# No-ops of the half pairs on four queues, later loads freed from the transposes, and a new order of steps

## The chip, the cores and the metric

The kernel runs on one core of a Trainium2 chip. A core has five engines with a queue of instructions each: TensorE (PE in the profile; its weight loads are listed apart as PEld), VectorE (DVE), ScalarE (ACT), GpSimd (POOL) and SyncE (SP). Here SP computes nothing: it issues transfers and holds no-ops. The metric is the time of one execution on the device, in microseconds. The profile's times count from the start of the span, the first instruction of the profiled execution; a clock of 1.00 is TensorE at full speed.

## What is computed

Two branches on the same normalised input, multiplied, and added to the input. S = 2048 tokens, D = 448, 16 heads of 28, F = 1792.

```
xn  = layernorm(x)                                  # no scale, no bias
q, k, v = heads of (xn @ wqkv)
idx = pos - 2 * (0 .. 7)                            # window 8, dilation 2
o   = softmax(q . k[idx] / sqrt(28), idx < 0 masked) @ v[idx]
s   = o @ wo                                        # branch A
f   = gelu(xn @ w1 + b1) @ w2 + b2                  # branch B
out = x + s * silu(f)
```

All inputs are bf16. A token attends only to tokens of its own parity.

## The kernel before

**Tiles and stages.** The tokens are split by parity into two halves of 1024 and cut into 16 tiles of 128: t0 to t7 are the even tokens, t8 to t15 the odd ones. Four tiles make one of the chunks c0 to c3, the 512 columns that a matmul of the hidden layer takes. Per tile: VectorE takes statistics of x_sb (line 353) and aggregates them; the inverse root follows (rstds; from t4 on on POOL, lines 374 and 375, two or four tiles at a time); VectorE normalises; and xn is turned into xnT, for t0 to t3 by TensorE, from t4 on by a transposing transfer that SP issues (dma_T, line 300). From xnT come Q and K of the tile (line 478), which are copied from a PSUM bank into qk_tok or qk_pair (line 251) and turned into qkT by another transposing transfer, and V (line 501), which POOL stores into v_rows in DRAM and loads back in strips for the attention (line 294). The hidden layer (ff1, line 551) takes one chunk of xnT and one of 14 column tiles of w1, m0 to m13; ACT applies gelu. The second layer (ff2) is line 577 for c0 to c2 and line 603 for c3. The attention works on nine blocks b0 to b8 of up to 228 tokens, each in two parts: keys (line 662), scores (line 677), exponential, mask (line 693), weighted sum of the values (line 708). The last part multiplies by wo (line 742), gates, adds x and stores.

**Pairs.** A contraction of 448 rows is three tiles of 128 and one of 64. The function pair takes two such jobs a and b with a PSUM bank each and runs their matmuls on the two row halves of the array at once: first a on rows 0 to 63 beside b on rows 64 to 127 (the first half of the pair), then with the row halves exchanged (the second half). Between the two stands a no-op on another engine's queue (line 437): it waits for the last matmuls of the first half, and the second half waits for it. So there are three steps: first half, no-op, second half. Before, the no-op is on POOL or on SP, and for pairs marked early (the projections and the hidden layer of c0 and c1) on POOL alone: 49 stand on POOL, 12 on SP.

**The order.** Every piece of work is a step of a plan (plan.add) with a number, the engines that may carry it, the steps that it depends on, and the buffers that it takes and gives back. emit walks through the string ORDER and issues the steps in its order. A word is an engine's letter and the step's number: P TensorE, V VectorE, A ACT, G POOL, S SP, D for a transfer's landing. Words of one letter are that engine's queue, which it works off in this order; buffers (the eight PSUM banks, the four buffers for xn among them) are handed out in the order of the words, so that a step can also wait for an earlier user of its buffer.

**Loads.** x comes in parts: t0, t1, t2 and t3, t4 to t7, and, by load_x(8, 4) and load_x(12, 4), t8 to t11 (step S256) and t12 to t15 (S258), 0.46 MB each. w2 comes in two halves, S262 and S260. These four depend on the issue of the xn transposes of t4 to t7 (the list turned, line 851), so that they stand behind them on SP's queue; so does the load of the bias b2 on POOL (G264).

**Steps that are spoken of.**
- Transposes on SP: S196, S200, S188, S192 turn xn of t6, t7, t4, t5; S137, S154, S144, S161 turn Q and K of t0, t2, t1, t3; S425 of t13.
- Pairs (first half, no-op, second half): V of t6 and t7 P239, 240, 241; Q and K of t4 P202, 203, P204, of t5 P209, 210, P211, of t6 P225, 226, P227, of t7 P232, 233, P234, of t10 P362, 363, P364, of t14 P436, 437, P438. Hidden layer of c0: P303, 304, P305 and P313, 314, P315, and further ones numbered 288 to 322. Hidden layer of c1: P472, 473, P474; P477, 478, P479; P482 and P502 are first halves of others, P487, P489, P497, P499 halves too. Second layer: P577, P579. The no-ops 217 and 340 belong to V of t4 and t5 and of t8 and t9, 444 to V of t14 and t15.
- Attention: scores P652, P657, P682, P687, P692; P782 is the weighted sum of b4, first part.
- VectorE: V281 is the statistic of t13, V229 the copy of Q of t6 out of its bank, V331 the normalisation of t10.
- POOL: G96 inverse root of t4 and t5; G278 and G287 those of t8 to t11 and of t12 to t15; G172 to G178 loads of values for b0, G180 and G182 for b1, G385 to G391 for b4; G357 the store of V of t8.

Of the kernel before, what the change touches and what calls it, by code (L numbers as in the profile page):

```python
# [11 lines left out]
ACT = mybir.ActivationFunctionType  # L12

HOPS = ("POOL", ("SP", "POOL"))
# [4 lines left out]
G98 P5 S40 D41 S44 D45 P6 S46 D47 P7 G100 P8 V58 P9 V59 S74 D75 V62 A60 P10 S76 D77 P11 V61 V102 P12 P13 G649 V103 P14  # L19
V63 P104 A64 P105 G27 V106 A107 D108 S78 D79 G28 V65 P128 G31 V109 G29 V110 G30 P111 P112 V113 S80 D81 P132 A114 D115  # L20
P129 S84 D85 V66 P184 P133 V67 V70 A68 S86 D87 P130 V69 V116 P131 V117 V71 V185 P118 V101 A72 P119 V99 A52 V120 D121
# [12 lines left out]
A685 G233 G661 V711 A584 P234 S363 V684 A242 P687 G920 G686 V236 P364 A235 V585 P586 A688 S237 D238 G243 D244 A690  # L34
V689 G246 D247 A581 G691 S921 D922 A366 V582 S923 D924 A365 P712 S367 D368 G587 P692 P662 V693 A713 P588 V663 V694
A715 V664 V695 V665 V696 V666 G697 D698 P346 V589 G667 D668 S669 D670 P717 V592 A590 G347 P671 G699 D700 P348 V672
A718 G252 D253 V673 P413 A349 G254 D255 V350 A720 P339 G414 V674 S351 D352 V675 A593 P415 G340 V740 G676 D677 P701
V714 A417 P341 G678 D679 V702 A416 V703 P595 A343 S418 D419 V716 V704 A342 V705 V741 G706 D707 S344 D345 V594 G708
D709 P722 V719 G596 P742 V723 P747 V724 A743 P597 S925 D926 A745 V725 V726 A748 V721 G727 D728 S729 D730 A750 V591
V744 V746 P731 V601 P376 V732 A602 V733 P369 G377 V734 P378 V735 G370 P353 V598 G738 S736 D737 D739 A382 S927 D928  # L40
V770 A599 P752 G383 D384 P371 V753 G354 V379 P355 A372 V754 G380 D381 P427 A356 V771 A359 P443 G357 D358 V755 V756
G360 D361 P772 V373 S444 S757 D758 P445 G428 G759 D760 A773 V749 S374 D375 P777 A775 V446 P429 A778 V751 P420 V800
# [3 lines left out]
A440 V784 V785 V786 G460 D461 G462 D463 V439 S789 G787 D788 D790 V806 S441 D442 G459 P807 V610 P537 A808 V607 A810  # L46
P791 S538 P812 V809 A54 G464 D465 P512 V792 V793 G466 D467 P539 V794 S513 V795 A608 P514 V813 G798 S796 D797 D799 V814
A541 S931 D932 P527 V815 A540 V816 P532 G528 V811 A515 G817 D818 V609 G819 D820 P821 A611 P529 V860 G533 G468 D469
A516 V822 P534 V823 G470 D471 A531 P507 V824 V825 A536 V612 P522 G826 D827 S828 D829 A530 G508 A535 P509 S523 A861
P517 P952 S518 A511 P524 G953 A510 S933 D934 P954 A525 P519 V955 A526 P941 V959 G956 A521 V960 P832 P837 A520 G942  # L50
S957 D958 P943 S961 D962 A55 P613 V944 V948 V949 A838 S950 D951 A840 V839 V945 A833 P862 V841 S946 D947 G614 P867 A835
V834 P615 A868 V836 A870 G869 A863 A865 V864 G871 A890 P842 V619 P622 G866 V843 V844 A620 V845 A891 V846 V616 G847
D848 V621 P851 G849 D850 A617 S623 P892 P624 V852 A893 V853 A895 V854 V855 V618 G856 D857 V894 G858 D859 V896 P547
V628 V625 P963 A629 G548 A626 V630 P897 G964 P974 A898 V627 A900 P965 V899 G975 A56 V901 P542 S935 D936 V970 P976 V971
G543 V966 S972 D973 P549 V977 G967 P902 A551 P544 V903 V904 S968 D969 A550 P552 V905 V978 A546 V906 S979 D980 P872
G553 P554 A545 V981 S907 D908 P881 S909 D910 V873 A556 P572 V874 A555 V882 P567 V883 S573 V884 V885 P574 S568 V875
G886 D887 P569 V876 A575 G888 D889 V982 P996 A576 G877 D878 S983 D984 P557 A571 G997 G879 D880 A570 P998 S558 P911
V999 P559 V912 P562 V913 A560 V1000 A561 P985 V914 S563 S1001 D1002 V915 P564 S937 D938 V1003 G986 G918 P987 V1004
A565 P631 S1005 D1006 V992 A566 S916 D917 D919 V988 A57 V993 P632 V989 S994 D995 S990 D991 P635 V633 A634 S939 D940
P1012 P636 P1007 V637 P639 A638 V1008 V1009 V1013 S1010 D1011 P640 G1014 P643 S1015 D1016 V641 A642 P644 P1022 A645  # L60
P1017 V1023 V1024 P646 V1018 S1025 D1026 P647 P1027 V1019 A648 V1028 S1020 D1021 V1029 S1030 D1031
# [61 lines left out]
def kernel(  # L123
# [12 lines left out]
    nc = tc.nc  # L136
    P = 128
# [795 lines left out]
```

## Time and profile before

| | us |
|---|---|
| three timed runs | 155.18, 153.72, 155.64 |
| their median | 155.18 |
| the profiled execution's own time | 155.25 |
| its span, first to last instruction | 153.6 |
| mean granted clock of TensorE | 1.000 |

The profile is of one execution. In its rows, L437 is a line of the kernel, an arrow points from the inputs to the output (out<-in), xN is a count. SPq and POOLq are the queues of SP and POOL, whose no-ops and issues of transfers are not counted as work. The busy time of the engines by stretch shows how the work is spread (the columns: start and end, length, busy us and instructions of each engine, TensorE's clock, mean busy share of the transfer engines, GB/s):

```
0.00:20.00 20.00, 18.00 (x130) 9.02 (x132) 15.57 (x58) 8.70 (x17) 10.30 (x38) 1.00 0.97 254
20.00:40.00 20.00, 18.40 (x176) 9.32 (x174) 10.07 (x31) 12.12 (x20) 7.94 (x13) 1.00 1.10 206
40.00:60.00 20.00, 18.14 (x262) 9.73 (x258) 14.39 (x33) 12.71 (x24) 11.45 (x15) 1.00 1.01 175
60.00:80.00 20.00, 20.00 (x370) 11.45 (x364) 19.01 (x51) 10.33 (x22) 8.28 (x15) 1.00 0.94 153
80.00:100.00 20.00, 18.86 (x298) 10.71 (x296) 17.71 (x49) 12.28 (x24) 13.16 (x23) 1.00 1.08 201
100.00:120.00 20.00, 20.00 (x304) 10.69 (x300) 12.96 (x30) 16.29 (x30) 7.83 (x11) 1.00 0.34 86
120.00:140.00 20.00, 20.00 (x248) 10.36 (x243) 15.48 (x37) 13.84 (x23) 3.61 (x6) 1.00 0.37 102
```

The five engines' columns are TensorE, its weight loads, VectorE, ACT and POOL. The last stretch, from 140.00 to 153.60, is not shown.

### The profile page before, as it was taken

Reading aid. Unit: us, or ns where it says so; the run is one execution under the profiler, and the core shown is the slowest. Engines: PE = TensorE matmul, PEld = TensorE weight load, DVE = VectorE, ACT = ScalarE, POOL = GpSimd, SP = SyncE. Lnnn points to the kernel's source line nnn. Section 1 sums busy time; section 2 is a strip of 40 time slices with the busy share of each in tenths; the row PEclk is TensorE's granted clock in tenths of the full one; section 3 lists DMA queues with packets and bytes.
Section 4 is the critical chain, followed back from the end, with each engine's and each line's share of the span. In section 5 each row is a group of like instructions: output and inputs, shape, how many; then the busy total and the mean of one; then the engine's idle time right before and its main releaser. Section 6 shows DMA issues by size and latency. Waiting matters only on the chain.

```text
span 153.6 us, 4656 instructions
## 1 busy us (share of the span) xinstructions
PE 143.6 (94%) x1828; PEld 77.4 (50%) x1828; DVE 110.2 (72%) x295; ACT 88.5 (58%) x161; POOL 63.6 (41%) x119
## 2 busy tenths in 40 slices
PE   6999999977999959999999889999999999999991
PEld 2554555533455526556555446545555555445560
DVE  5689962068845795999999959925869999481542
ACT  3253576693485574374367227998895775672120
POOL 6833396002918490453274864742084022210200
PEclk9999999999999999999999999999999999999999
DMA  4999999999599898979689999981601242353301
GB/s 145 343 329 287 165 200 153 277 227 258 103 230 178 164 157 188 113 182 156 143 109 275 136 174 224 227 192 22 180 0 41 57 107 68 101 145 90 89 30 60
DMA packets 43950, 24.28 MB, mean 158 GB/s; under 512 B 33778, under 2 KB 41978, under 8 KB 43928
## 3 DMA queue, kind: packets, MB, share of 16 engines
q1 hardware_dynamic: 41080, 17.25, 58.7%
q0 software_dynamic: 2704, 6.62, 17.8%
q8 instruction: 14, 0.23, 0.7%
q10 hardware_dynamic: 144, 0.11, 0.2%
q14 instruction: 8, 0.07, 0.2%
HBM read 9.82 MB, written 6.29 MB: 105 GB/s over the span
## 4 chain that ended last, share of the span: by engine, by line
PE 64%; DMA 17%; DVE 11%; POOL 2%; issue 2%; SPq 1%; ACT 0%; POOLq 0%; DVEq 0%
PE bank L551 16%; PE bank L577 16%; PE bank L478 8%; PE bank L603 7%; DMA xnT<-xn 6%; PE bank L742 5%; DMA x_sb<-in_A_x_dram 5%; PE bank L501 4%; DMA v<-v_rows 4%; PE bank L264 3%; PE bank L708 3%; DVE kb L662 3%; DVE st L353 3%; DMA qkT<-qk_pair 2%; PE bank L677 2%
## 5 line engine op out<-in xcount | busy, mean ns | idle before, releaser
L551 PE MATMUL bank<-xnT,w 64*128 64x512 bf16 x392 | 47.3, 376 | 0.8 <-DVE qk_tok L251 0.8
L555 ACT ACTIVATE h<-bank,b 128x512 bf16<-128x512 f32 x56 | 35.2, 685 | 16.4 <-PE bank L551 16.0
L577 PE MATMUL bank<-w,h 64*128 64x448 bf16 x336 | 33.7, 349 | 0.0
L551 PEld LDWEIGHTS <-w 64*128 64x128 bf16 x392 | 20.3, 94 | 20.6 <-issue 1.8
L478 PE MATMUL bank<-w_in,xnT 64*128 64x448 bf16 (+1 forms) x212 | 26.8, 352 | 3.6 <-SPq L437 2.6
L683 ACT ACTIVATE E<-bank 128x456 bf16<-128x456 f32 (+1 forms) x36 | 17.4, 550 | 12.3 <-PE bank L677 10.2
L731 POOL DMA_DIRECT2D o_rows<-a x25 | 13.4, 540 | 25.1 <-DVE a L724 10.0
L577 PEld LDWEIGHTS <-h 64*128 64x128 bf16 x336 | 16.1, 94 | 13.9
L724 DVE TENSOR_TENSOR a<-bank,rd 114x448 bf16<-114x448 f32 (+1 forms) x36 | 22.2, 622 | 1.1
L294 POOL DMA_DIRECT2D v<-v_rows x22 | 13.6, 627 | 10.6 <-DMA v_rows<-v_tok 6.0
L478 PEld LDWEIGHTS <-xnT 64*128 64x128 bf16 (+1 forms) x212 | 10.3, 94 | 12.7 <-SPq L437 2.8
L353 DVE BATCH_NORM_STATS2 st<-x_sb 128x6 f32<-128x448 bf16 x16 | 9.5, 612 | 8.2 <-DMA x_sb<-in_A_x_dram 8.2
L501 PE MATMUL bank<-w_in,xnT 64*128 64x448 bf16 (+1 forms) x106 | 14.1, 351 | 0.0
L619 DVE TENSOR_TENSOR y<-bank,b 128x448 f32<-128x448 f32 x15 | 9.0, 621 | 6.3 <-PE bank L603 4.8
L294 POOL DMA_DIRECT2D v_rows<-v_tok x16 | 9.2, 576 | 7.4 <-DVE v_tok L251 4.6
L603 PE MATMUL bank<-w,h 128*128 128x448 bf16 (+2 forms) x70 | 11.4, 315 | 0.0
L693 POOL TENSOR_TENSOR E<-E,m_gen 128x456 bf16<-128x456 bf16 x8 | 8.5, 1076 | 6.4 <-ACT E L683 6.4
L631 ACT ACTIVATE t<-y 128x448 f32<-128x448 f32 x12 | 6.9, 579 | 7.2 <-DVE y L619 7.2
L662 DVE TENSOR_SCALAR kb<-qkT,plane 128x512 bf16<-128x512 bf16 x30 | 10.7, 410 | 0.2 <-DMA qkT<-qk_pair 0.2
L773 POOL TENSOR_TENSOR o<-x_sb,sg 128x448 bf16<-128x448 bf16 x3 | 3.1, 1030 | 17.8 <-DVE sg L767 9.1
L387 DVE TENSOR_SCALAR xn<-x_sb,mv,rstd 128x448 bf16<-128x448 bf16 x16 | 6.2, 396 | 5.8 <-DMA xnT<-xn 3.5
L693 DVE TENSOR_TENSOR E<-E,m_gen 128x456 bf16<-128x456 bf16 (+1 forms) x24 | 9.1, 391 | 1.4 <-ACT E L683 1.4
(80 smaller groups left out, 178.7 us busy)
## 6 DMA issues: line engine op xcount, KB each, us to landing
v_rows<-v_tok POOLq DMA_DIRECT2D x16, 128.0 KB, 4.0
v<-v_rows POOLq DMA_DIRECT2D x14, 128.0 KB, 4.3
out_dram<-o SPq DMA_DIRECT2D x15, 112.0 KB, 1.7
w<-in_B_w_dram SPq DMA_DIRECT2D x2, 784.0 KB, 14.4
o_rows<-a POOLq DMA_DIRECT2D x23, 64.1 KB, 2.7
w<-in_B_w_dram SPq DMA_DIRECT2D x2, 672.0 KB
x_sb<-in_A_x_dram SPq DMA_DIRECT2D x3, 448.0 KB, 6.2
w_in<-in_A_wqkv_dram SPq DMA_DIRECT2D x3, 336.0 KB, 3.9
```

Of the source, the lines that this page charges most:

```text
L294: nc.gpsimd.dma_start(dst(k), src())
L353: nc.vector.bn_stats(out=buf(p_st, k)[:], in_=x_sb[:, t, :])
L478: return nc.tensor.matmul(ps[:, :D], xnT[r, kt, cs], w, start=start, stop=stop)
L501: return nc.tensor.matmul(ps[:, :D], xnT[r, kt, k0:k0 + P], w, start=start, stop=stop)
L551: return nc.tensor.matmul(ps[:], w1[r, kt, ms], xnT[r, kt, cs], start=start, stop=stop)
L555: nc.scalar.activation(buf(p_h, own, i)[:], buf(p_b, own, i)[:], ACT.Gelu_apprx_tanh, bias=b1[:, mt:mt + 1])
L577: return nc.tensor.matmul(ps[:, :D], buf(*h_at[(c, mt)])[r, j * P:(j + 1) * P], w2[r, mt, :], start=start, stop=stop)
L603: nc.tensor.matmul(ps[:, :n], buf(*h_at[(c, mt)])[:, j * P:(j + 1) * P], w2[:, mt, cs], start=(mt == 0 and not biased), stop=(mt == NMT - 1))
L662: nc.vector.tensor_scalar(dst, src, plane[:, e:e + 1], None, op0=ALU.mult)
L683: nc.scalar.activation(buf(p_E, k)[:, :n], buf(p_b, a, r)[:, :n], ACT.Exp, scale=SCALE)
L693: (nc.gpsimd if k.on == "POOL" else nc.vector).tensor_tensor(out=E, in0=E, in1=m, op=ALU.mult)
L724: nc.vector.tensor_tensor(out=o, in0=sums(k, e)[:, :, :, :DH], in1=buf(p_rd, rd)[rows].unsqueeze(2).unsqueeze(3).to_broadcast((2 * nq, 8, ...
```

## The change

The no-op of any pair may stand on POOL, SP, ACT or VectorE; the mark early is gone. The loads of x for t8 to t15 and of w2 no longer depend on the transposes of t4 to t7; the load of b2 still does. ORDER is replaced as a whole. With it:
- 38 no-ops stand on POOL, 13 on SP, 6 on ACT (A299, A319, A444, A543, A573, A997) and 4 on VectorE (V217, V340, V473, V563). No-ops 451, 478, 508 and 964 go from POOL to SP; 363 and 437 stay on SP.
- S258 stands ahead of S137, S256 ahead of S154, S262 behind the transposes of t4 to t7, S260 some 30 words later.
- Seven copies out of banks (142, 206, 212, 245, 373, 379, 423) go from VectorE to ACT, 430 the other way; one key step (800) goes from VectorE to ACT. Of the masks, 659 and 871 go to VectorE, 684, 749, 806, 841 and 901 to POOL. Of the issues of stores of attention rows, 759, 768, 817, 879 and 886 go from POOL to SP, 766 and 789 from SP to POOL. The last addition of t11 (1004) goes from VectorE to POOL.
- The order on every engine is another. No step is added or left out.

```diff
-HOPS = ("POOL", ("SP", "POOL"))
+HOPS = ("POOL", "SP", "ACT", "DVE")
...
-S88 D89 P134 V73 V122 P149 V123 V136 A135 V146 P124 G150 P125 A139 P151 S137 D138 V126 D127 G147 D148 V142 P293 G140
-D141 V152 P298 V153 G294 V94 S154 D155 P163 G299 V92 P295 V93 G164 V95 V90 G97 P300 A297 V143 P165 V82 A302 S144 D145
-P313 V194 A166 V198 A296 V195 G167 D168 P308 V199 S196 D197 V83 V91 V169 G314 G96 A301 P315 S200 D201 P303 A316 G309
-V186 G170 D171 V187 V190 A317 G172 D173 P310 V191 S188 D189 G304 G174 D175 P156 V650 A311 G176 D177 V651 P305 A312
-S192 D193 G157 G178 D179 P158 A307 P288 V159 A160 S258 D259 G264 D265 S256 D257 A306 P318 G289 S262 D263 G180 D181
-S260 D261 P290 G319 G182 D183 P225 A291 P320 A292 G226 P227 A322 P482 V281 A321 V283 S161 D162 P502 A228 G483 V284
-V229 P484 G503 V279 P492 A485 V270 V276 A486 P504 G493 V277 V280 P494 V272 A506 P472 V282 V273 A505 V274 V275 A495
-P209 V271 G473 V285 G278 A496 P474 V286 P216 G210 V331 G287 A475 V332 V335 S333 D334 P211 A476 V336 V327 P477 G217
-G268 D269 V213 S337 D338 G266 D267 V212 P218 V323 G478 P487 A219 V324 V328 S214 D215 A222 G220 D221 P479 G488 G223
-D224 V680 P489 A481 S329 D330 V681 P497 A490 V409 A480 P202 V410 S325 D326 G498 A491 V397 P499 G203 V398 S399 D400
-P204 A501 P652 V205 P577 A500 S411 D412 V206 A53 G248 D249 V405 G250 D251 V406 S207 D208 A653 V401 P239 A655 G578 V402
-G654 S407 D408 P579 G240 G656 S230 D231 S403 D404 P657 V583 P682 A658 P241 V580 A660 G659 P232 V245 A683 P362 V710
-A685 G233 G661 V711 A584 P234 S363 V684 A242 P687 G920 G686 V236 P364 A235 V585 P586 A688 S237 D238 G243 D244 A690
...
-A780 P761 V774 A447 G421 P422 V762 G385 D386 A430 V763 S448 D449 P450 G387 D388 A433 V764 V765 G389 D390 P604 A424
-V423 G451 S766 D767 G391 D392 S929 D930 V776 G393 D394 V801 G395 D396 V603 G431 D432 S425 D426 V600 G434 D435 P452
-V779 G605 P436 V781 G768 D769 A456 V453 P802 G457 D458 V830 S437 P438 A803 G454 D455 V831 P782 A805 P606 G804 V783
...
+P129 S84 D85 V66 P184 P133 V67 V70 A68 P130 V69 S86 D87 V116 P131 V117 V71 V185 P118 V101 A72 P119 V99 A52 V120 D121
+P134 V73 V122 P149 V123 V136 S88 D89 A135 V146 P124 G150 S258 D259 P125 A139 P151 V126 D127 G147 D148 A142 V143 S137
+D138 P293 G140 D141 V152 P298 V153 G294 S256 D257 V94 P163 A299 V92 P295 V93 G164 V95 V90 G97 P300 A297 V82 S154 D155
+P165 A302 V83 G172 D173 V194 P313 V198 A166 G174 D175 V195 V199 S196 D197 V91 A296 V169 P308 G96 A301 V281 P318 S200
+D201 G314 V186 G309 G167 D168 V187 P315 V190 G170 D171 A319 V191 V279 P310 S188 D189 G176 D177 A316 V280 G178 D179
+P156 V282 V283 A311 S192 D193 P320 V284 A317 V285 G157 P288 V286 A312 G287 S144 D145 V270 A322 P158 V276 A321 P303
+G289 G264 D265 V159 S262 D263 A160 G180 D181 V277 P290 V272 G304 G182 D183 P305 V273 V274 A291 P225 V275 A307 V271
+V409 G278 V397 P239 A306 V398 V410 A292 P232 G226 G240 S161 D162 P227 G233 V331 P202 V229 A228 V332 P234 G203 P204
+V335 P502 V336 V205 A206 P492 G503 V650 A235 V651 P504 G493 V236 P494 A506 P482 A505 S260 D261 A495 P209 S333 D334
+G483 A496 P484 G210 G268 D269 P472 A485 G266 D267 A486 P211 V473 P474 V213 A212 P216 V680 A475 S214 D215 V681 P487
+A476 V217 P218 G488 P477 S207 D208 A219 A222 G220 D221 P489 V327 S478 G223 D224 S399 D400 P497 V328 A490 A491 P479
+G498 S329 D330 P499 A481 P652 A480 S337 D338 P241 A501 P577 G248 D249 S237 D238 A500 G250 D251 A53 S411 D412 P682 A653
+G578 V323 P579 S230 D231 V324 A655 G654 V405 A683 V406 A685 G684 S325 D326 V401 V402 A242 A245 G686 P657 S407 D408
+V583 P362 A658 V580 G656 A660 P692 P687 G920 S363 V693 S403 D404 A584 P364 V694 G661 A581 P586 V710 A688 V695 V696
...
+P420 V446 A447 V776 P450 S448 D449 G421 G385 D386 V430 A433 P761 G387 D388 P422 V762 G389 D390 S451 V763 S929 D930
+P452 A424 G391 D392 V764 P777 V765 A456 P436 G393 D394 V453 A778 S768 G395 D396 P604 S437 V830 A423 G431 D432 V779
+A780 S425 D426 G434 D435 V831 G454 D455 V781 G766 D767 D769 G457 D458 P802 P782 A803 P438 G605 V783 V784 A805 G804
...
-    def pair(a, b, early=False, n1=4, n2=3, after=(), give=()):
+    def pair(a, b, n1=4, n2=3, after=(), give=()):
...
         def f2(k):
-            held["told"] = (nc.gpsimd if k.on == "POOL" else nc.sync).nop()
+            held["told"] = {"POOL": nc.gpsimd, "SP": nc.sync, "ACT": nc.scalar, "DVE": nc.vector}[k.on].nop()
             for i in held["last"]:
                 behind(held["told"], i)
-        told = plan.add(HOPS[0] if early else HOPS[1], f2, [t])
+        told = plan.add(HOPS, f2, [t])
...
     turned = [t_xT[t].deps[0] for t in range(TPC, 2 * TPC)]
-    load_x(8, 4, "SP", turned)
-    load_x(12, 4, "SP", turned)
-    t_w2 = [[dma("SP", w2[:, 7 * i:7 * i + 7, :], B_w2[F // 2 * i:F // 2 * (i + 1), :].rearrange("(m p) c -> p m c", p=P),
-                 turned)] for i in range(2)]
+    load_x(8, 4, "SP")
+    load_x(12, 4, "SP")
+    t_w2 = [[dma("SP", w2[:, 7 * i:7 * i + 7, :], B_w2[F // 2 * i:F // 2 * (i + 1), :].rearrange("(m p) c -> p m c", p=P))] for i in range(2)]
     t_b2 = dma("POOL", b2[:], B_b2.rearrange("(o d) -> o d", o=1).to_broadcast((P, D)), turned)
```

More of the change, by code (lines that the diff above doesn't have):

```diff
@@ L37 @@
[L37 to L41, printed above, removed]
@@ L47 @@
[L47 to L51, printed above, removed]
@@ L52 @@
[L52 to L61, printed above, removed]
+G98 P5 S40 D41 S44 D45 P6 P7 G100 S46 D47 P8 V58 P9 V59 S74 D75 V62 A60 P10 S76 D77 P11 V61 V102 P12 P13 G649 V103 P14
@@ new lines @@
+A748 P731 A750 V744 G749 P597 V732 A382 V733 A379 G383 D384 V734 V735 A800 G380 D381 V746 S927 D928 G738 V770 P752
+V771 P353 S736 D737 D739 V601 P369 G354 V598 A602 P355 V753 A599 G370 V754 P427 A356 V755 V756 A359 P371 G357 D358
+V751 S757 D758 G360 D361 P772 V801 S759 D760 A373 P443 G428 V603 A372 P429 V600 A444 S374 D375 A773 P445 A775 V774
+P420 V446 A447 V776 P450 S448 D449 G421 G385 D386 V430 A433 P761 G387 D388 P422 V762 G389 D390 S451 V763 S929 D930
+P452 A424 G391 D392 V764 P777 V765 A456 P436 G393 D394 V453 A778 S768 G395 D396 P604 S437 V830 A423 G431 D432 V779
@@ L62 @@
+D991 P636 P1007 V637 P643 A638 V1008 V1009 P644 V1013 S1010 D1011 G1014 P639 A645 S1015 D1016 P640 P1022 V641 P1017
+V1023 A642 V1024 P646 V1018 S1025 D1026 P647 P1027 V1019 A648 V1028 S1020 D1021 V1029 S1030 D1031
 """
@@ L583, in ff2_pair @@
         last = j == TPC - 2
-        t_f2[t] = pair(job(t), job(t + 1), False, NMT, NMT, [t_f2[t - 2]] if last else (),
+        t_f2[t] = pair(job(t), job(t + 1), NMT, NMT, [t_f2[t - 2]] if last else (),
                        tuple(h_at[(c, mt)] for mt in range(NMT)) if last else ())
@@ L831, in project @@
                 for n in range(2):
-                    pair(*js[n], c < 2)
-                pair(vs[2 * i], vs[2 * i + 1], c < 2)
+                    pair(*js[n])
+                pair(vs[2 * i], vs[2 * i + 1])
         if c == NCH - 1:
@@ L869 @@
         for i in range(0, NMT, 2):
-            pair(hs[i], hs[i + 1], c < 2)
+            pair(hs[i], hs[i + 1])
         if c == 0:
```

27 lines of the change are left out of this document (20 added, 7 removed).

## The prediction

> **What bounds the kernel now.** I read the page first, then the waits of TensorE, then the order of time around each of them, then the chain of waits.
>
> ```profile
> span 153.6 us, 4656 instructions
> ...
> PE 143.6 (94%) x1828; PEld 77.4 (50%) x1828; DVE 110.2 (72%) x295; ACT 88.5 (58%) x161; POOL 63.6 (41%) x119
> ```
>
> TensorE works 143.6 of 153.6 us, so only 10.0 us can be had without taking matmuls away, and the change takes none away. The waits say who holds those microseconds (in all, times, longest):
>
> ```profile
> PE bank L478 <- SPq L437: 2.6, 2, 1.9
> ...
> PE bank L478 <- POOLq L437: 0.8, 1, 0.8
> PE bank L551 <- DVE qk_tok L251: 0.8, 1, 0.8
> PE bank L708 <- DMA v<-v_rows: 0.4, 1, 0.4
> ```
>
> Line 437 is the no-op between the halves of a pair. Together these are 4.6 us behind the start-up. Four places follow, with start, length and, in brackets, the idle time before. The first two have one cause:
>
> ```profile
> 18.81 5.40 SPq L300 DMA_TRANSPOSE xnT<-xn  x4
> 24.26 1.17 SPq L287 DMA_DIRECT2D x_sb<-in_A_x_dram  x2
> 25.48 4.34 SPq L287 DMA_DIRECT2D w<-in_B_w_dram  x2
> 29.93 8.22 SPq L300 DMA_TRANSPOSE qkT<-qk_pair  x1
> ```
>
> ```profile
> 24.05 0.62 DVE L251 CAST qk_pair<-bank 128x448 bf16<-128x448 f32 x1 [0.74 <-PE bank L478]
> 31.94 1.15 DVE L353 BATCH_NORM_STATS2 st<-x_sb 128x6 f32<-128x448 bf16 x2 [7.26 <-DMA x_sb<-in_A_x_dram]
> 33.22 0.59 DVE L251 CAST qk_tok<-bank 128x448 bf16<-128x448 f32 x1
> ```
>
> ```profile
> 33.87 1.02 PE L551 MATMUL bank<-xnT,w 64*128 64x512 bf16 x7 [0.79 <-DVE qk_tok L251]
> ...
> 37.85 0.74 PE L478 MATMUL bank<-w_in,xnT 64*128 64x448 bf16 x6 [0.81 <-POOLq L437]
> ```
>
> ```profile
> 37.44 0.30 POOL L374 TENSOR_SCALAR sd<-mv,eps_t 128x4 f32<-128x4 f32 x1 [10.52 <-DVE mv L357]
> 37.83 1.04 POOL L375 TENSOR_TENSOR rstd<-sd,half_t 128x4 f32<-128x4 f32 x1
> ```
>
> The x loads of the second half go out at 24.26, behind the last transposes of xn. VectorE stands 7.26 us before V281, the first statistic on them. Behind V281 waits the copy V229 (33.22), which frees the bank that P472 needs: 0.79. Behind the same statistics waits the POOL step G278 (37.44), and behind that no-op G210, which P211 needs: 0.81. The third place:
>
> ```profile
> 54.22 0.39 PE L677 MATMUL bank<-qkT,kb 64*128 64x57 bf16 x16
> 56.47 0.74 PE L478 MATMUL bank<-w_in,xnT 64*128 64x448 bf16 x6 [1.86 <-SPq L437]
> ```
>
> ```profile
> 46.69 3.07 SPq L300 DMA_TRANSPOSE xnT<-xn  x2
> 49.85 1.26 SPq L300 DMA_TRANSPOSE qkT<-qk_pair  x1
> 51.20 1.24 SPq L300 DMA_TRANSPOSE xnT<-xn  x1
> 52.54 2.51 SPq L300 DMA_TRANSPOSE qkT<-qk_tok  x1
> 55.14 1.22 SPq L300 DMA_TRANSPOSE xnT<-xn  x1
> ```
>
> SP issues transposes one behind the other; no-op S363 stands behind the one of 55.14, and P364 waits 1.86. The fourth:
>
> ```profile
> 86.26 2.22 SPq L300 DMA_TRANSPOSE qkT<-qk_pair  x1
> ...
> 88.59 0.74 PE L478 MATMUL bank<-w_in,xnT 64*128 64x448 bf16 x6 [0.72 <-SPq L437]
> ...
> 89.77 0.39 PE L708 MATMUL bank<-v,E 64*128 64x58 bf16 x15 [0.42 <-DMA v<-v_rows]
> ```
>
> P438 waits 0.72 for no-op S437, which stands behind transpose S425 (2.22), and P782 then 0.42 for values. Matmul ends are modelled: the group at 54.22 is given 0.39, but in the chain of waits such a group is followed after 0.22, so each bracket is 0.17 short. The places are worth 0.96 and 0.98, 2.03, and 0.89 and 0.59: 5.45 us.
>
> ```profile
> 57.21 2.65 PE bank L577 x28
> ...
> 59.86 0.22 PE bank L677 x16
> ...
> 63.17 0.76 PE bank L478 x8
> ...
> 93.03 0.86 PE bank L551 x8
> ```
>
> These four are the prices of TensorE's steps below; a second half of 6 matmuls costs three quarters of a first half of 8, 0.57 and 0.65.
>
> **The change part by part.** *The x loads.* S258 moves to where SP had nothing to do, ahead of transpose S137, and S256 right behind it, ten or more us before 24.26. The loads' landing no longer decides V281, and the statistics fall into VectorE's idle 7.26. Eight statistics and aggregates are moved, none added. Gain: both stops, 0.96 + 0.98 = 1.94. The cover is that the loads stand ahead of four xn transposes (S196, S200, S188, S192) on the same queue. The last of these is issued at about 22.9 (18.81 plus three quarters of 5.40) and lands by the median below at 27.3. In the order before, the step at 26.20 is Q and K of tile 6, and the first hidden-layer pair that needs all four tiles stands 0.76 + 0.65 + 0.57 behind it, at 28.2. The new order puts P239, P232, P202 (0.76 each), P234 and P204 (0.57 each) ahead of that pair, 3.4 us, so it is due at 31.6. The loads may hold the transposes for 4.3 us free of charge.
>
> ```profile
> 17.97 4.06 PE L551 MATMUL bank<-xnT,w 64*128 64x512 bf16 x36
> ...
> 26.20 0.94 PE L478 MATMUL bank<-w_in,xnT 64*128 64x448 bf16 x8
> ```
>
> ```profile
> xnT<-xn SPq DMA_TRANSPOSE x12, 4.4
> ...
> v_rows<-v_tok POOLq DMA_DIRECT2D x16, 128.0 KB, 4.0
> ```
>
> *The no-op S363.* In the new order SP carries no-op S478, eight transposes and then S363. S478 waits for P477, so the eight start when P477 has ended. TensorE has from there to P364: P489, P479, P499 at 0.65, P497 0.86, P241 0.57, P577 and P579 at 2.65, P362 0.76, and P652, P682, P657, P692, P687 at 0.22: 10.5 us. Eight transposes at 1.35 (5.40 by 4) are 10.8; at 1.61 (46.69 to 56.36 for six) 12.9. P364 waits 0.3 to 2.3 us in place of 2.03. I take 0.5, near the row of four, since the 2.51 is one outlier of six: gain 1.5, between -0.3 and 1.7.
>
> *The no-op S437* now stands ahead of S425: the 0.89 goes. But P782 is late next. Its values come by a row of POOL transfers (copy, store G357, loads G385 to G389) that the change leaves as they are, with the same TensorE work beside them. Gain of the two together: 0 to 1.48; I take 0.6, below the middle, since that chain gets no shorter.
>
> *POOL's queue.* Two places get worse.
>
> ```profile
> 13.41 1.17 POOL L294 DMA_DIRECT2D v_rows<-v_tok  x2 [4.06 <-DVE v_tok L251]
> ...
> 19.68 0.30 POOL L374 TENSOR_SCALAR sd<-mv,eps_t 128x2 f32<-128x2 f32 x1
> 20.06 0.72 POOL L375 TENSOR_TENSOR rstd<-sd,half_t 128x2 f32<-128x2 f32 x1
> ...
> 21.37 1.83 POOL L294 DMA_DIRECT2D v<-v_rows  x3
> ```
>
> The value loads G172 and G174 move ahead of G96 and no-op G314. They wait for the stores of 13.41 to land, by the median 4.0 at about 18.0, take 0.61 each, and G314 follows G96's first operation at about 19.6. P315 needs it at 17.97 + 3 x 0.86 = 20.5. So it is free with 0.9 to spare; each us that the stores land later than 18.9 stops TensorE for one. And no-op G304 now stands behind G287 (0.30 and 1.04), the bias load G264 and value load G180 (0.6 each). G287 needs the last of four statistics behind norm t5; from about 22.0 these take 2.6 us, so G304 comes at about 26.9, and P305 is due where 26.20 was: 0.7. Price of the two: 0 to 3.0; I take 0.7.
>
> *No-ops on ACT and DVE.* Six and four. What waits behind each needs, nearly always, a later TensorE step anyway; tight are V217, V340 and A444, whose second half is due 0.4 to 0.9 behind the first. How a no-op stands to work ahead of it on its own engine is seen on POOL alone:
>
> ```profile
> L437 POOLq EVENT_SEMAPHORE  x1: 17/17/17, 20.0 to 20.0; - x1
> ```
>
> It fired at 20.0, before the operation of 20.06 ahead of it had run. So an operation ahead costs nothing if it has been handed over; bounds 0 and about 0.6 a place; I take 0. The Trainium skill, "PSUM — Partial Sum Buffer", Engine vs sequencer instructions, says the same of all engines: a no-op waits for what is ahead to be dispatched, not done. The row agrees; were it otherwise, the three tight places would give up to 1.8 us, and the sum would be 153.7.
>
> *Sum.* -1.94 - 1.5 - 0.6 + 0.7 = -3.3 us, on this execution's own 155.25 (span 153.6 and 1.65 around it; 0.07 above the median 155.18 of 153.72 to 155.64): 151.9. Over 2% is 3.1 us, about what a measurement of this kernel can tell from no change.
>
> **The rivals.** *Later stops take the gain back.* The transposes keep the pace of 1.61 and the value chain its time, so that only the x loads' 1.94 is won and POOL's 0.7 paid: 154.0. For it: neither chain is shortened. Against: the outlier.
>
> *The loads hold the transposes.* At 29.93 one transpose behind four loads held SP for 8.22 against 1.24, 7.0 too long. The new order puts two of those loads ahead of the xn transposes that TensorE needs next. Above 4.3 us it decides: at 7.0 the hidden-layer pair waits 2.7, V331, which needs their buffer, again holds V229, so that the 1.94 is not won; all later transposes on SP are late too, so nothing of the 1.5 and 0.6 either; with POOL's 0.7: 158.7. Against it: the two are 0.9 of the 2.4 MB that stood there, 2.6 us in proportion, under 4.3. The Trainium skill, "DMA: Bandwidth & Descriptors", Queues, rings and completion order, speaks for it: descriptors are consumed in ring order on each DMA engine, so a load ahead is served first. The row of 29.93 agrees.
>
> *It does not do what it says.* The loads could be issued early and land no sooner. SP was free ahead of S137 and the queue served only what stood before, so I give this no chance of its own.
>
> **How the numbers follow.** Forecast, 151.9: 0.45, its own range 149.8 (all 5.45 won) to 153.4. Gain taken back, 154.0: 0.35. Transposes held, 158.7: 0.20. These are also faster, same and slower; the forecast stands close to the border, so some of the first case may fall into the second and the reverse. The range goes from 148.8 (all won, and a run 1.0 below) to 158.2 (nothing won, POOL's price at 3.0); it leaves out most of the slower case.
>
> **What would show it.** Right: no wait of VectorE for x_sb, no stop at 33.9 and 37.9; P364 stopped under 1 us by SP's no-op; a stop near 20.5 or 26.2 by POOL's no-op, under 1 us together. Wrong: TensorE waiting for xnT's transposes near 31; SP's no-op still 2 us late; a wait for values over 1.5 us; a stop at a no-op of ACT or DVE.

## The result and the profile after

| | before | after |
|---|---|---|
| median of 4 runs, us | 155.41 (153.72 to 155.84) | 163.27 (162.20 to 164.41) |
| profiled execution, us | 155.25 | 162.20 |
| its span, us | 153.6 | 160.5 |
| mean granted clock of TensorE | 1.000 | 0.979 |

The changed kernel is slower: 1.053 of the time before, interval 1.041 to 1.065. The forecast was 151.9. Ratios here leave disturbed runs out, while medians are over all runs, so that in a short row of runs the two can differ by a per cent.

The page of the changed kernel, first lines:

```profile
span 160.5 us, 4651 instructions
...
PE 146.1 (91%) x1828; PEld 83.5 (52%) x1828; DVE 105.3 (66%) x283; ACT 92.4 (58%) x169; POOL 66.2 (41%) x120
```

TensorE runs the same 1828 matmuls and is busy 2.5 us longer (146.1 for 143.6). The waits of TensorE (in all, times, longest):

```profile
PE bank L551 <- POOLq L437: 3.2, 1, 3.2
PE bank L708 <- DMA v<-v_rows: 2.0, 1, 2.0
PE bank L551 <- DVE qk_tok L251: 1.9, 1, 1.9
...
PE bank L478 <- SPq L437: 1.3, 1, 1.3
PE bank L757 <- DMA oT<-o_rows: 0.7, 1, 0.7
```

These are 9.1 us where the four lines that were quoted of before gave 4.6. So 4.5 more of waiting and 2.5 more of work make 7.0, and the span grew by 6.9. The longer work is the clock. Stretches of half a microsecond around the first stop, and of one around the stop for values (the columns: start and end, length, TensorE's busy us, its granted clock, share of the transfer engines, GB/s):

```profile
22.00:22.50 0.50, 0.00 (x0) 1.00 0.90 201
22.50:23.00 0.50, 0.00 (x0) 0.52 1.29 286
23.00:23.50 0.50, 0.26 (x2) 0.50 1.32 251
...
25.50:26.00 0.50, 0.50 (x6) 0.56 0.85 238
26.00:26.50 0.50, 0.50 (x8) 1.00 0.77 166
...
93.00:94.00 1.00, 0.20 (x14) 1.00 1.17 175
...
95.00:96.00 1.00, 1.00 (x8) 0.50 1.47 127
...
98.00:99.00 1.00, 1.00 (x19) 1.00 1.24 344
```

TensorE's last matmul ahead of the first stop ended at 20.07. At about 22.5 its clock fell to half, and it came back at about 25.9, 2.7 us after the work had begun again at 23.24. Matmuls issued meanwhile take double. The same happens after the stop for values (half from 94.2 to 97.6).

Where the first two stops come from is read from the other engines' order of time, first POOL, then VectorE:

```profile
12.75 1.17 POOL L294 DMA_DIRECT2D v_rows<-v_tok  x2 [3.51 <-DVE v_tok L251]
15.84 0.30 POOL L374 TENSOR_SCALAR sd<-mv,eps_t 128x2 f32<-128x2 f32 x1 [1.93 <-DVE mv L357]
16.23 0.72 POOL L375 TENSOR_TENSOR rstd<-sd,half_t 128x2 f32<-128x2 f32 x1
21.52 1.27 POOL L294 DMA_DIRECT2D v<-v_rows  x2 [4.56 <-DMA v_rows<-v_tok]
22.81 0.31 POOL L374 TENSOR_SCALAR sd<-mv,eps_t 128x2 f32<-128x2 f32 x1
```

```profile
18.42 0.62 DVE L353 BATCH_NORM_STATS2 st<-x_sb 128x6 f32<-128x448 bf16 x1
...
39.23 1.15 DVE L662 TENSOR_SCALAR kb<-qkT,plane 128x512 bf16<-128x512 bf16 x4 [2.73 <-DMA qkT<-qk_pair]
40.30 0.62 DVE L251 CAST qk_tok<-bank 128x448 bf16<-128x448 f32 x1
```

```profile
23.24 2.74 PE L551 MATMUL bank<-xnT,w 64*128 64x512 bf16 x12 [3.17 <-POOLq L437]
...
40.97 1.02 PE L551 MATMUL bank<-xnT,w 64*128 64x512 bf16 x7 [1.88 <-DVE qk_tok L251]
```

POOL stands 4.56 us before the value loads G172 and G174, until the stores of 12.75 have landed. Behind them wait G96 (22.81) and no-op G314, and TensorE goes on at 23.24. On VectorE V281 starts at 18.42 without waiting for x, as forecast (31.94 before). But the key steps V650 and V651 (39.23) wait for a transpose into qkT, and behind them stands V236 (40.30), which frees the bank that P482 needs.

### The profile page after: what moved, and what is told of

It reads as the page before. It is cut to its first block, busy times and chain, and to the rows that moved or that the text cites. A ratio compares the mean times of both kernels' runs of the same rounds, so it can differ in the third digit from the quotient of the medians.

```text
span 160.5 us, 4651 instructions
## 1 busy us (share of the span) xinstructions
PE 146.1 (91%) x1828; PEld 83.5 (52%) x1828; DVE 105.3 (66%) x283; ACT 92.4 (58%) x169; POOL 66.2 (41%) x120
## 4 chain that ended last, share of the span: by engine, by line
PE 62%; DMA 20%; DVE 10%; issue 3%; POOL 2%; SPq 0%; DVEq 0%; POOLq 0%
PE bank L577 19%; PE bank L551 15%; PE bank L478 9%; DMA qkT<-qk_pair 6%; DMA v_rows<-v_tok 5%; PE bank L603 5%; PE bank L501 4%; DMA v<-v_rows 4%; DMA oT<-o_rows 3%; PE bank L742 3%; DMA o_rows<-a 3%; PE bank L264 3%; PE bank L677 2%; PE bank L708 2%; DVE a L724 2%
## 5 line engine op out<-in xcount | busy, mean ns | idle before, releaser
L551 PE MATMUL bank<-xnT,w 64*128 64x512 bf16 x392 | 49.0, 384 | 5.1 <-POOLq L437 3.2
L577 PE MATMUL bank<-w,h 64*128 64x448 bf16 x336 | 35.3, 359 | 0.0
L551 PEld LDWEIGHTS <-w 64*128 64x128 bf16 x392 | 22.3, 95 | 24.5 <-issue 4.2
L577 PEld LDWEIGHTS <-h 64*128 64x128 bf16 x336 | 19.3, 97 | 12.6 <-issue 1.6
L724 DVE TENSOR_TENSOR a<-bank,rd 114x448 bf16<-114x448 f32 (+1 forms) x36 | 22.5, 624 | 1.2
L731 POOL DMA_DIRECT2D o_rows<-a x22 | 11.7, 535 | 15.7 <-DVE a L724 5.0
L693 POOL TENSOR_TENSOR E<-E,m_gen 128x456 bf16<-128x456 bf16 x11 | 11.6, 1072 | 10.0 <-ACT E L683 9.3
L773 POOL TENSOR_TENSOR o<-x_sb,sg 128x448 bf16<-128x448 bf16 x4 | 4.1, 1030 | 16.9 <-DVE sg L767 9.5
L662 DVE TENSOR_SCALAR kb<-qkT,plane 128x512 bf16<-128x512 bf16 x28 | 8.8, 366 | 3.0 <-DMA qkT<-qk_pair 2.7
```

Source lines behind the costliest of these rows:

```text
L551: return nc.tensor.matmul(ps[:], w1[r, kt, ms], xnT[r, kt, cs], start=start, stop=stop)
L577: return nc.tensor.matmul(ps[:, :D], buf(*h_at[(c, mt)])[r, j * P:(j + 1) * P], w2[r, mt, :], start=start, stop=stop)
L693: (nc.gpsimd if k.on == "POOL" else nc.vector).tensor_tensor(out=E, in0=E, in1=m, op=ALU.mult)
L724: nc.vector.tensor_tensor(out=o, in0=sums(k, e)[:, :, :, :DH], in1=buf(p_rd, rd)[rows].unsqueeze(2).unsqueeze(3).to_broadcast((2 * nq, 8, ...
L731: (nc.gpsimd if k.on == "POOL" else nc.sync).dma_start(o_rows[n + i * nq:n + i * nq + nq, :], buf(p_a, own)[i * nq:i * nq + nq, i, :])
```

## The experiments

Each is the new or the old order of words with the words shown moved; the computation is whole in all of them. Groups that were run together share their runs of the kernel before: medians 153.67 for the first four, 154.30 for the value loads alone, the keys early, the w2 load and the repaired order, 154.31 for both parts in the old order, POOL's fault, the ten no-ops and the row of b4, 154.64 for VectorE's fault and SP's order, 154.03 for the first mask. In some of them the order takes one line less, and the line numbers are lower by one (L550 for L551).

**The value loads behind the no-ops.**

```diff
-V83 G172 D173 V194 P313 V198 A166 G174 D175 V195
+V83 V194 P313 V198 A166 V195
...
-G314 V186 G309 G167
+G314 V186 G309 G172 D173 G174 D175 G167
```

> The new order with one edit: the value loads G172 and G174 stand behind the no-ops G314 and G309 on POOL, in place of ahead of them. Theory (POOL's queue): the stop of 3.36 us at P315 goes, and with it the half clock that follows it (0.61 + 0.64 us), so 4.6 us less than the changed kernel's 163.3: 158.7, and the clock near 20 to 26 us stays 1.00. Rival (the early x loads hold the xn transposes, and POOL's stop only hid that): TensorE stops at the first hidden-layer pair of chunk 1 (P502) for transposes of xn instead, and less than 2 us are gained: above 161.3.

Measured 164.07 (163.10 to 165.57), ratio 1.068: no gain, though the mechanism was right. Its waits:

```profile
PE bank L550 <- DVE qk_tok L250: 5.5, 1, 5.5
PE bank L707 <- DMA v<-v_rows: 2.2, 1, 2.2
```

POOL's stop is gone from the list, and the stop behind V650 has grown from 1.9 to 5.5, with a half clock behind it. V650 started at 39.05 here and at 39.23 in the changed kernel, though S161 was issued at 25.96 here and at 29.61 there: the second stop ends at a time that the transfers fix, so what the first one gives back the second one takes. The two could not be read as a sum.

**The keys behind the bank copy.**

```diff
-V650 A235 V651 P504 G493 V236 P494
+A235 P504 G493 V236 V650 V651 P494
```

> The new order with one edit: the two key steps V650 and V651 of the first block stand behind the bank copy V236 on VectorE, in place of ahead of it. Theory (VectorE's queue): V650 waits for the transposes of tile t3 (S161), which landed at 39.19 behind the w2 load, and held V236, which frees the bank that P482 needs; without it the stop of 2.07 us at 38.8 goes: 161.2. Rival (the bank is late for another reason, or the stop reappears at the next step that needs these transposes): 162.5 or more.

Measured 158.10 (156.30 to 160.84), ratio 1.021. The stop behind V650 is gone. The four runs fall in two pairs: 156.30 and 156.62 at a clock of 0.998, 159.59 and 160.84 at 0.978. In the profiled one, at 0.979, the half clock followed POOL's stop of 2.1 and the stop of 2.0 for values; the others were not profiled.

**Both.** The two diffs above together.

> Both edits together, G172 and G174 behind the no-ops and V650 and V651 behind V236. If the two stops are independent: 163.3 - 4.6 - 2.1 = 156.6, with the stops at S363 (1.5), at the values of block b4 (2.2 and the half clock behind it, 1.4) and at oT (0.9) left as they are. Rival: what the two stops covered comes up in their place (the transposes of xn at P502, w2 at P577), 158.5 or more.

Measured 156.89 (155.63 to 159.21), ratio 1.021 against 1.053 for the change, and by the ratio no better than the keys alone (1.021). The profile has no half clock, and it shows what stood behind the two stops: POOL's queue once more, now at no-ops G157 and G304.

```profile
24.63 0.74 PE L477 MATMUL bank<-w_in,xnT 64*128 64x448 bf16 x6 [0.89 <-POOLq L436]
...
26.39 0.82 PE L550 MATMUL bank<-xnT,w 64*128 64x512 bf16 x6 [0.15 <-POOLq L436]
28.42 0.82 PE L550 MATMUL bank<-xnT,w 64*128 64x512 bf16 x6 [1.21 <-POOLq L436]
```

**The early x loads alone, in the old order.**

```diff
-S137 D138
+S258 D259 S137 D138
...
-S154 D155
+S256 D257 S154 D155
...
-S258 D259 G264 D265 S256 D257 A306
+G264 D265 A306
```

> The old order with one part of the change: the x loads S258 and S256 go out early, ahead of the Q and K transposes S137 and S154. Theory: the two stops behind the late x loads (0.98 and 1.17) go, 153.3, since in the old order no value load stands ahead of an early pair's no-op; the store of v_rows lands about 2.4 us later (21.3 in place of 18.9) and harms nothing before 24 us. Rival (the loads hold the xn transposes): the hidden-layer pair P482, due at 28.2, waits 1 to 2 us for xnT, 154.3 to 155.5, or more where the whole row of transposes is late.

Measured 156.94 (156.09 to 157.47), ratio 1.022: the rival holds, with a longer stop and a longer time than it gave. The two stops behind the late x are gone, and in their place TensorE waits for xnT and then runs at half clock:

```profile
31.52 2.74 PE L550 MATMUL bank<-xnT,w 64*128 64x512 bf16 x12 [2.74 <-DMA xnT<-xn]
```

**The value loads alone, in the old order.**

```diff
-G314 G96 A301
+G172 D173 G174 D175 G314 G96 A301
```

> The old order with one edit: the value loads G172 and G174 stand ahead of no-op G314 on POOL, as in the new order. Theory (the value loads do harm only where the stores of v_rows land late, which the early x loads bring about): the stores land at 18.9, the two loads take 1.2 us, G314 fires at 20.1 in place of 20.0; no change, within 0.5 us of before. Rival (the place of the value loads alone is the fault): a stop of 2 us or more at P315, 156 to 158.5.

Measured 154.31 (152.89 to 157.30), ratio 1.002 (0.997 to 1.008): no change, as the theory said. On POOL the value loads went out at 19.56 after a wait of 0.28:

```profile
13.05 1.17 POOL L293 DMA_DIRECT2D v_rows<-v_tok  x2 [3.92 <-DVE v_tok L250]
...
19.56 1.23 POOL L293 DMA_DIRECT2D v<-v_rows  x2 [0.28 <-DMA v_rows<-v_tok]
```

**Both parts in the old order.**

> The old order with two parts of the change at once: the x loads early, and the value loads G172 and G174 ahead of no-op G314. Alone, the first cost 3.3 us on the medians (a stop for xnT), the second nothing. Theory (the stores of v_rows land late because of the x loads, and only then the value loads hold the no-ops): G172 goes out at 20.3 to 22, G314 about 1.2 us later, TensorE stops 1.3 to 3.5 us at P315 with the half clock behind it where the stop is over 2.1; the stop for xnT behind it is partly covered by that: 157.5 to 161. Rival (no such coupling): 156.9, as with the x loads alone, and no stop at P315.

Measured 158.69 (155.98 to 159.30), 4.4 over the median of before, where the x loads alone were 3.3 over theirs. The value loads went out at 22.35, and the stop is there; no wait for xnT is listed any more beside it:

```profile
PE bank L551 <- POOLq L437: 3.6, 1, 3.6
```

So in the old order the place of the value loads costs nothing with late x loads, and 3.6 us of waiting with early ones; the new order with late x loads was not run. From store to value load it is 6.5 us without the early x loads (13.05 to 19.56) and 8.8 in the changed kernel (12.75 to 21.52). In the seven profiles with early x loads in which only the landing held the value loads it is 6.7 to 9.5, and they started between 19.96 and 22.35. So POOL's stop is not the same each time: it is 1.1, 2.1, 3.2 and 3.9 in the four profiles with the changed kernel's words on POOL.

**The keys early.**

```diff
-G240 S161 D162
+G240 V650 V651 S161 D162
...
-V650 A235 V651 P504
+A235 P504
```

> The new order with one edit: the key steps V650 and V651 stand ahead of the transpose S161 of tile t3 in the order, in place of behind it; V236 stays behind them. In the plan they need only the transposes of t0 and t1. Theory (a key step waits for every transpose into qkT that stands ahead of it in the order, whichever tile it is of): V650 now waits only for those of t0, t2 and t1, which landed at 30.4, the stop of 2.07 us at 38.8 goes, and the time is that of the run with the keys behind V236, 156.3 to 160.8. Rival (V650 was late for t1's transpose or by its place on VectorE): the stop stays, 162 or more.

Measured 157.98 (155.63 to 160.18), ratio 1.018. V650 ran at 34.04 without a wait, and P482 did not stop. The keys of the first block hold no token of t3, and the step waits for S161 only when S161 stands ahead of it in the order; here S161 in its turn waited 5.1 us for V650. The plan's list doesn't have this dependence. That it comes from the layout of qkT, over which the strips are read with a stride, is likely but was not tried.

**The w2 load behind S161.**

```diff
-V159 S262 D263 A160
+V159 A160
...
-S161 D162 P227
+S161 D162 S262 D263 P227
```

> The new order with one edit: the first w2 load S262 is issued behind the transpose S161 in place of ahead of it, so that one w2 load less stands in front of S161 on the transfer queues. Theory (S161 landed at 39.2, 9.5 us behind its issue, because of that load): S161 lands near 32, V650 and V236 follow, the stop at 38.8 goes: 156.3 to 161.2. Rival (S161 is slow for another reason, the value loads and the bias load on POOL's queue): it still lands at 37 or later, and the time stays at 162 or more.

Measured 159.48 (157.17 to 161.05), ratio 1.027. V650 started at 36.07 in place of 39.23, not near 32, and a stop of 1.5 stayed. But the transpose ahead, S144, was already 1.6 us earlier in this run (25.64 for 27.20) and S161 2.2 us (27.43 for 29.61); from its issue to V650 it is 8.6 us for 9.6. With the load ahead of it, it is 13.1 with the value loads behind the no-ops (25.96 to 39.05), and 8.2 with VectorE's fault put back further down (26.20 to 34.40). So this run doesn't show that the load ahead holds S161; what does stays open. POOL's stop was only 1.1 in this run, with the same words in POOL's queue as the changed kernel: the stores landed earlier, the value loads went out at 19.96.

**A repaired order.** The keys behind V236, and, each line showing one engine's words alone:

```diff
-G172 G174 G96 G314 G309 G167 G170 G176 G178 G157 G287 G289 G264 G180 G304 G182 G278 G226
+G96 G314 G309 G167 G170 G157 G172 G174 G289 G176 G178 G304 G287 G226 G278 G264 G180 G182
...
-S325 S407 S363
+S363 S325 S407
...
-P632 P1012 P635
+P632 P635 P1012
```

> The new order with the keys behind V236, and further: on POOL the no-ops G314, G309, G157, G289 and G304 ahead of the value loads or between them, with the stores G167 and G170 first and the inverse roots, the b2 load and the later value loads behind G304; on SP the transposes S325 and S407 behind no-op S363; on TensorE P1012 behind P635. Theory: of the stops that the run with both edits shows, 1.1 + 0.3 + 1.4 (POOL's no-ops), 1.5 (S363) and 1.2 (oT) go, 5.5 us, 156.9 - 5.5 = 151.4, faster than before by 1 to 2%. Rival (the xn transposes and w2 behind the early x loads are late next): a stop for xnT or w2 of 2 us or more, 153.5 or more.

Measured 152.10 (150.86 to 154.68, 12 runs), ratio 0.990 (0.985 to 0.994): 1% faster than the kernel before. Its waits that are left, the first weights' and three later ones:

```profile
span 150.8 us, 4652 instructions
...
PE bank L708 <- DMA v<-v_rows: 0.8, 1, 0.8
PE bank L478 <- DMA w_in<-in_A_wqkv_dram: 0.5, 1, 0.5
PE bank L708 <- DVE E L693: 0.4, 1, 0.4
...
PE bank L677 <- DVE kb L662: 0.3, 1, 0.3
```

No wait for xnT is left: with the new order of TensorE the xn transposes behind the early x loads are in time. This kernel served to put single parts back.

**POOL's fault put back.**

```diff
-G96 G314 G309 G167 G170 G157 G172 G174 G289
+G172 G174 G96 G314 G309 G167 G170 G157 G289
```

> The repaired new order with the value loads G172 and G174 put back to where the change has them, ahead of G96 and no-op G314. Theory (POOL's queue is the first cause): a stop of 1.3 to 4 us at P315, as in the runs that had this order (3.4, 2.3, 4.1, 1.3), and the half clock behind it where it is over about 2.1 us; 152.1 + 1.3 to 5.4, 153.4 to 157.5. Rival (with the other stops gone the value loads find their cover again): 152.1 within 0.8.

Measured 157.51 (156.82 to 158.37), ratio 1.026: 5.4 us for the place of two loads. All four runs have a clock of 0.988 or 0.989.

```profile
PE bank L551 <- POOLq L437: 3.7, 2, 3.1
```

The longest wait is 3.1, and the matmuls behind it lost 1.3 to the half clock (TensorE is busy 144.8 for 143.5).

**VectorE's fault put back.**

```diff
-V236 V650 V651 P494
+V650 V651 V236 P494
```

> The repaired new order with the key steps V650 and V651 put back ahead of V236, where the change has them. Theory (VectorE's queue is a second cause of its own, which POOL's stop had partly covered): V650 starts when S161 has landed, at 34 to 38.5, V236 1.1 us later; P482, due at 34.8 in the repaired order, waits for its bank until then, 1 to 4.5 us, with the half clock (1.3 to 1.6) behind a stop over about 2.1: 153.1 to 158. Rival (with POOL's queue mended S161 lands in time): 152.1 within 0.8.

Measured 153.42 (151.55 to 156.79), ratio 0.988 (0.979 to 0.998) against its own runs of before. The stop is in the trace, below the length that brings the half clock; four runs don't resolve a price of this size.

```profile
34.40 1.15 DVE L662 TENSOR_SCALAR kb<-qkT,plane 128x512 bf16<-128x512 bf16 x4 [2.05 <-DMA qkT<-qk_pair]
...
36.13 1.02 PE L551 MATMUL bank<-xnT,w 64*128 64x512 bf16 x7 [1.20 <-DVE qk_tok L251]
```

**SP's order put back.** S325 and S407 ahead of S363 again.

> The repaired new order with the transposes S325 and S407 put back ahead of no-op S363, where the change has them. Theory (the row of eight transposes behind no-op S478 takes longer than TensorE's work up to P364): a stop of 1.1 to 1.6 us at P364, as in the runs that had this order, 153.2 to 153.7. Rival (prediction's value): 0.5 us, 152.6 or less.

Measured 153.74 (151.88 to 154.89), ratio 0.986 (0.977 to 0.995). Undecided: in the profiled run another stop, 2.0 us for a bank, stood right ahead of P364 and hid whatever S363 would have cost.

**The ten no-ops of ACT and VectorE on POOL.** Letters only: G299, G319, G444, G543, G573, G997, G217, G340, G473, G563.

> The repaired new order with the ten no-ops that the change put on ACT and VectorE (A299, A319, A444, A543, A573, A997, V217, V340, V473, V563) on POOL's queue in the same places of the order. Theory (a no-op's queue costs nothing of itself, as the rows of the ten show no stop behind them): 152.1 within 0.8. Rival (POOL is crowded, which is what the other queues are for): a no-op waits behind a value load or a mask on POOL, 153.5 or more.

Measured 152.89 (151.62 to 155.69, 12 runs), ratio 0.997 (0.992 to 1.002): within the 0.8 of the theory, but not quite where the repaired order stands. The one long stop of its profile is not at a no-op. VectorE, POOL and TensorE in order of time:

```profile
48.71 4.98 DVE L392 COPY xn<-xn 128x64 bf16<-128x64 bf16 x1
53.61 1.14 DVE L619 TENSOR_TENSOR y<-bank,b 128x448 f32<-128x448 f32 x2
```

```profile
48.59 1.06 POOL L693 TENSOR_TENSOR E<-E,m_first 128x456 bf16<-128x456 bf16 x1
49.60 2.05 POOL L693 TENSOR_TENSOR E<-E,m_gen 128x456 bf16<-128x456 bf16 x2
51.61 1.04 POOL L693 TENSOR_TENSOR E<-E,m_first 128x456 bf16<-128x456 bf16 x1
52.61 1.03 POOL L693 TENSOR_TENSOR E<-E,m_gen 128x456 bf16<-128x456 bf16 x1
```

```profile
54.28 0.40 PE L677 MATMUL bank<-qkT,kb 64*128 64x57 bf16 x16 [2.12 <-DVE y L619]
```

V402, a copy of 64 columns, takes 4.98 us, from the start of POOL's first mask to the end of its fifth, and the bank that TensorE needs is freed behind it. It is the stop in the profile of SP's order put back as well, where V402 also took 4.98.

**The first mask on VectorE.**

```diff
-A655 G654 V405
+A655 V405
...
-V402 A242
+V402 V654 A242
```

> The repaired new order with the first mask of block b0 (654) moved from POOL to VectorE, right behind the copy V402. In two runs of repaired orders V402, a copy of 64 columns that takes 0.18 us elsewhere, took 4.98 us, from the start of POOL's first mask to the end of its fifth, and TensorE stopped 2.0 to 2.1 us for the bank that VectorE frees behind it; in three others V402 ended as the first mask began and nothing stopped. Theory (a POOL mask and such a copy keep each other out, and POOL's row of masks does not let the copy in between): with POOL's row starting behind V402, V402 takes 0.18 us in the profile and the runs of 154 and more become rare, median 151.9, of the 12 or so runs at most one over 154 other than by the clock. Rival (the long copy has nothing to do with the masks): the long copy or the runs over 154 stay, 2 or more of 12.

Measured 152.30 (151.77 to 155.94, 12 runs), ratio 0.989 (0.985 to 0.993). Ten of the runs lie between 151.77 and 152.89; one is over 154 at full clock (155.29), one with the clock at 0.989 (155.94). V402 took its 0.18, and POOL's masks began behind it:

```profile
48.63 0.18 DVE L392 COPY xn<-xn 128x64 bf16<-128x64 bf16 x1
48.72 0.39 DVE L693 TENSOR_TENSOR E<-E,m_first 128x456 bf16<-128x456 bf16 x1
```

That agrees with the theory. It is no proof by count: the repaired order had two of twelve over 154.

**The row to the values of b4 begun earlier.**

```diff
-P597 P752 P353 P369 P355 P427
+P353 P597 P355 P752 P369 P427
...
-A800 A602 A599 A356 A359
+A800 A356 A359 A602 A599
...
-G383 G380 G738 G354 G370 G357 G360
+G354 G383 G380 G738 G357 G360 G370
```

> The repaired new order, with the row that ends in the values of block b4 begun earlier: on TensorE P353 ahead of P597 and P355 ahead of P752, on ACT the copies A356 and A359 right behind, on POOL the stores G357 and G360 ahead of no-op G370, about 2 us earlier. Theory (P782 waits for that row, 0.97 us in the repaired order): the stop goes, 151.1. Rival (the transposes on the same transfer queues decide when the value loads land): the stop stays, 152.1.

Measured 154.02 (152.38 to 157.62, 12 runs), ratio 1.003 (0.997 to 1.009): worse than the repaired order, so the theory fails.

```profile
PE bank L708 <- DMA v<-v_rows: 4.8, 3, 2.9
```

The stores of t8 and t9 were begun 1.5 us earlier (74.48 for 75.97), but the value loads went out when they had in the repaired order (79.67 for 79.88), and landed later. On POOL they now wait for TensorE, no longer for the stores:

```profile
79.67 3.62 POOL L294 DMA_DIRECT2D v<-v_rows  x6 [4.12 <-PE bank L478]
```

The no-op G421 of another pair stands right ahead of them on POOL's queue and fired at 79.0 (79.3 in the repaired order). The edit moved the stores and left that no-op where it was. Why the loads then landed later was not tried.

## Why the prediction was wrong

**POOL's queue: the step that failed.** The prediction saw both places, G314 behind the value loads and G304 behind G287 and its followers, and took 0.7 for the two, between 0 and 3.0. Three things were wrong with that sum.
- The landing of the stores was taken as the median of all sixteen, 4.0. They were issued while the loads of the start still moved 396 GB/s (12 to 14 us, value loads alone), and even without the early x loads the value loads behind them start 6.5 us after the stores (13.05 to 19.56). The median of a row is no price for its worst-placed instruction.
- The x loads and the value loads were priced apart. The place of the value loads costs nothing with late x loads (1.002), and 3.2 us of waiting in the changed kernel. The prediction even gave the rule, each us past 18.9 stops TensorE for one, and then did not ask what the change itself does to that landing: it puts 0.9 MB of loads beside the stores. The runs in the old order show the coupling: no wait at POOL's no-op beyond 0.5 us with either part alone, 3.6 with both.
- A stop of that length also halves the clock for 3.4 us, 1.3 us more, a cost that the prediction has nowhere. With that the place alone costs 5.4 in the repaired order, over the upper bound of 3.0.

**VectorE's queue: not seen.** V650, V651 and V236 were moved on VectorE and against S161, and no step of the prediction priced them: it followed the no-ops, the loads and the statistics. The changed kernel waits 1.9 there, and 5.5 where POOL's stop is mended alone.

**The values of b4.** The prediction took 0.6 of gain for S437 and P782 together, with 0 as the worst. S437's stop did go: no wait behind it is in the list. But the wait for values rose from 0.4 to 2.0 with a half clock behind it, so the pair cost. The value loads go out 0.6 to 0.7 us behind no-op G421 (which fires at 82.1 before, at 85.7 in the changed kernel), and their values are there 7.0 and 7.4 us after that issue. TensorE got to P782 7.2 us behind the no-op before, 6.1 in the changed kernel: 0.7 of the difference is S437's stop, which had covered a part of the landing. So the two were no sum of gains, and the lower end should have been below nothing.

**S363.** A wait of 0.5 was taken, with 0.3 to 2.3 as bounds; it is 1.3 in the changed kernel, 0.9 to 1.3 in the five variants of the new order that kept SP's order. The mechanism was right. In the changed kernel's order of time of SP, and of TensorE, the first of the eight transposes and the matmuls behind the no-op are:

```profile
48.63 4.07 SPq L300 DMA_TRANSPOSE xnT<-xn  x3
```

```profile
60.46 0.74 PE L478 MATMUL bank<-w_in,xnT 64*128 64x448 bf16 x6 [1.34 <-SPq L437]
```

Eight took from 48.63 to about 60.4, 1.47 each, between the two paces that were quoted. Put back alone it was not settled.

**Right.** The x loads: VectorE no longer waits at V281, and the stops of 0.96 and 0.98 are in no run with early x loads. The cover of 3.4 us by P239, P232 and P202: in the old order, which lacks it, the loads do stop TensorE for xnT (2.74), and in the new order they don't. So the slower rival named a real mechanism and the right sign, but not the place. The no-ops on ACT and VectorE: no second half waits for one of the ten in any profile, and the ratio with all ten on POOL is 0.997, for 0.990 in the repaired order, whose profile lacks the stop behind V402.

**The sum.** The changed kernel's profiled execution is 9.7 longer than that of the repaired order (162.20 to 152.51). Its listed waits are 9.1 for 2.0 (0.8 + 0.5 + 0.4 + 0.3), 7.1 more, and TensorE is busy 2.6 longer (146.1 for 143.5), which is the clock. Against before, by the lists of waits and in the prediction's terms: the x loads gave 1.6 and S363 0.6; S437 with P782 cost 0.9, POOL's queue 3.2, VectorE's 1.9, a wait for oT 0.7 that no term had, and the half clock 2.5. These make the 7.0.

## What to carry to other kernels

When a transfer is moved earlier, list what lands in the same stretch, and ask for each landing which instruction stands on an in-order queue behind its wait; the instruction that pays is often a no-op for another engine. Price a stop of TensorE of about 2 us or more with the half clock added, here 1.3 to 1.7 us where that lasted 3.4 us, 2.0 and 2.7 in the two places where it lasted 6.8; near 2 us it depends on where the stop falls (below). And when one stop is mended and the time stays, look where the next stop ends: if that is a fixed time, such as a landing, both must be mended before either shows.

## What the runs showed of the hardware

**The clock falls after short stops.** In these profiles TensorE's clock fell to half in eleven places, behind stops of 1.95 us and more, and stayed there 3.41 us, in two of them 6.8. Where one profile has two falls, the second comes 21.0, 20.0 and 17.0 times 3.41 us after the first (22.52 and 94.20 in the changed kernel): the falls lie on a grid that runs through the kernel. Stops of 1.86, 1.88, 2.00 and 2.12 were followed by full clock. Each of these lies across a point of its grid (read from the other falls, or from the fall behind the end of the execution), with at most 1.4 us in one interval, while each of the eleven has 1.95 or more in one. This is read from the traces; no run moved a stop to try it. The Trainium skill, "TensorE: Matmul & The Clock Gate", Part 1: The HAM clock gate, has the clock fall after an idle window of about 3.4 us that runs freely. The grid agrees with the window and its length. It does not agree that the whole window must be idle: 1.95 us in it was enough, and five of the falls came after the work had begun again, the latest 1.3 us after.

**A VectorE copy lasted through five POOL instructions.** In two profiles V402 took 4.98 us in place of 0.18 beside a row of five masks. The Trainium skill, "SBUF — State Buffer", SBUF: two separate sides, says that the port pair that the two engines share goes to the one that starts first for its whole instruction. The rows agree with the exclusion, and show more: POOL's row of masks went through without the copy coming in between. It is not so each time: with the keys behind the bank copy V402 stood beside the same row of five masks, began 0.12 us behind the first (52.67) as well, and ended with it.

```profile
52.79 0.98 DVE L391 COPY xn<-xn 128x64 bf16<-128x64 bf16 x1
```

What makes the difference was not tried.
